# A PSUM pool chosen tile by tile, with a new order of the second part of the program, in a gated linear attention followed by a low-rank mixer

## The chip, the cores and the metric

One core of a Trainium2 chip runs the whole program. The metric is the device time of one execution in microseconds. TensorE (PE in the profile, with its weight loads shown apart as PEld), VectorE (DVE), ScalarE (ACT) and GpSimd (POOL) each take their instructions in program order; SyncE (SP) does nothing but issue transfers, in program order too.

## The reference

Two stages in float32, batch 4, 768 tokens, 8 heads of 48. The first is a gated linear recurrence with a complex gate per channel; the second adds a low-rank mix over the tokens and then a two-layer network with a ReLU.

```python
for t in range(S):                                   # S = 768
    new_re = ar * S_re - ai * S_im                   # ar, ai: normalized gates of token t
    new_im = ar * S_im + ai * S_re
    kv = einsum('bhd,bhe->bhde', k[:, :, t], v[:, :, t])
    S_re, S_im = (new_re + kv, new_im)
    y[:, :, t] = einsum('bhd,bhde->bhe', q[:, :, t], S_re)

x  = y as (B, S, 384)
u  = x + (x^T @ U @ V)^T                             # U 768x32, V 32x768
ch = maximum(u @ w_ch1, 0.0) @ w_ch2                 # 384 -> 1536 -> 384
return u + ch
```

## The kernel before

**Attention.** The tokens are cut into 24 chunks of 128 (6 for each batch), two chunks to a group, and each chunk into two halves of 64 rows (`HC`). What a token gains or loses through the gates is made once for a group: magnitudes and angles on ACT and DVE, sums over tokens as matmuls with constant triangles (`ef ps`, `es ps`, L692; `ph`, L799; `tot`, L744). Then, for each chunk:

- `prep` (L843) weighs q and k, and PE transposes them (`tr`, L866); ACT copies the transposes out of PSUM (L877).
- `chain` (L888) has the scores within blocks of 32 tokens (`inner`, L913 and L916). DVE selects them by masks (L928, into a tile named `DG`), and four transfers that SP issues put the four diagonal blocks into the score matrix `AT` (L964). PE adds the scores across blocks (`corners`, L977), copied by ACT (L982).
- `dk` (L1002) is what the chunk adds to the state `G`; DVE scales and adds it (`onward`, L1008).
- `y` is scores times values (`inside`, L1033, which needs the four transfers) plus queries times state (`before`, L1041).

Four more transfers (L724) lay a group's totals out as `T`; they are issued by SP too.

**Mixer.** Twelve mixers work on two chunks each: `rank` (L1076) and `mixed` (L1095) are the low-rank mix, `uTp` (L1113) the transposes. The first layer is `up` (L1128) in the first three mixers and in the others `few` (L1228), 15 products in place of 18, in groups of 8 matmuls, added together by ACT and DVE (L1236, L1240). The second layer is `down` (L1319 in the first, L1362, seven products in place of eight, in groups of 6, in the others), with the sums by DVE at L1354 and L393. `leave` (L1298) writes the result out.

**How a matmul lies on the array.** Most groups load the whole 128x128 array: `few`, `down`, `up`, `uTp`, `rank`, the sums over tokens. The others load a part: `inside` and `dk` 64x64 pieces, `tr` and `mixed` two halves of 64 rows, `inner`, `corners` and `before` strips of 96 rows by 16, 32 or 64 columns. The argument `way` of a group names this.

**The order.** The body of the program does not issue its operations as it goes. It calls `plan.add` for each (through `PE`, `DVE`, `ACT`, `SP`, `POOL`), and `Plan.order` (L218) sorts all 2770 operations by a table, `ORDER`, that gives each its position. The table has a row for each engine and kind of operation and a list for each chunk, group or mixer, so it sets what stands next to what on every engine, and with that the order of SP's transfers (kinds `load`, `totals` and `place`). Waits between the engines follow from the data and from the buffers.

**PSUM.** There are four pools of two banks: `psT`, `psA`, `psY`, `psM`. Every PSUM tile is taken from one of them, in turn, and the tile that takes a bank waits until the tile two back in the same pool has been read. The pool of a tile is given by its kind: sums over tokens, `rank`, `mixed`, `uTp` and half the transposes in T, `inner`, `corners` and the other half in A, `dk` and most `y` in Y, `up` and `down` in M, and `few` in Y or M for its two long sums and A or T for the rest. The whole program has 479 such tiles.

Of the kernel before, what the change touches and what calls it, by code (L numbers as in the profile page):

```python
# [16 lines left out]
PSUM = bass.MemoryType.PSUM  # L17
# [11 lines left out]

ORDER = {  # L30
# [28 lines left out]
        ('DVE', 'gates'): {0: [5, 8, 13, 18, 19, 54, 49], 1: [30, 21, 40, 43, 44, 51, 50], 2: [111, 143, 156, 185, 169], 4: [277, 322, 323, 372, 356],  # L59
# [10 lines left out]
        ('ACT', 'angles'): {0: [72, 86, 98, 100, 103], 1: [76, 106, 112, 114, 126], 2: [210, 231, 251, 240, 241, 242, 263, 269, 271], 4: [375, 395,  # L70
# [5 lines left out]
        ('DVE', 'angles'): {0: [81, 89], 1: [87, 107], 2: [211, 232, 252], 4: [376, 402, 425], 6: [589, 596, 601, 611, 624, 625, 664], 8: [697, 714,  # L76
# [4 lines left out]
        ('DVE', 'prep'): {0: [85, 104, 110], 1: [121, 128, 145], 2: [226, 250, 265], 3: [203, 304, 309], 4: [373, 424, 427], 5: [443, 470, 472], 6:  # L81
# [6 lines left out]
        ('ACT', 'prep'): {0: [115, 117, 120, 122], 1: [158, 147, 154, 160], 2: [266, 270, 283, 281], 3: [319, 320, 327, 318], 4: [442, 439, 446, 445],  # L88
# [4 lines left out]
        ('DVE', 'rest'): {0: [118, 149, 155, 175, 159, 170, 194], 1: [174, 229, 234, 259, 209, 235, 248, 253], 2: [288, 315, 325, 366, 291, 314, 324,  # L93
# [79 lines left out]
        ('POOL', 'small'): {0: [790, 789], 1: [1213, 993, 1219], 2: [1414, 1280, 1404], 3: [1712, 1508, 1563], 4: [1901, 1754, 1798], 5: [2048, 2010,  # L173
        2037], 6: [2388, 2121, 2330], 7: [2427, 2408, 2409], 8: [2591, 2517, 2557], 9: [2692, 2645, 2657], 10: [2723, 2711, 2745]},
        ('POOL', 'angles'): {6: [614], 8: [706, 731], 10: [875, 913], 12: [1074], 14: [1226, 1309], 16: [1482, 1564], 18: [1745], 20: [1942, 1978],
        22: [2251, 2287]},
        ('DVE', 'mixing'): {3: [868, 1004, 892, 1043, 1073, 822, 1255, 1044, 1266, 1275, 1286, 1298, 1290]},
}
# [1412 lines left out]
```

## Time and profile before

| | |
|---|---|
| time, median of 3 runs | 622.64 us (622.42 to 623.75) |
| the profiled execution | 622.64 us, of which its span 620.9 us |
| granted TensorE clock | 1.00 |
| busy: PE / PEld / DVE / ACT / POOL | 97% / 85% / 86% / 65% / 6% |

The span is what the profile shows, from the first instruction to the last; 1.74 us of the profiled time lie around it. PE is the engine that is busy nearly all the time; DVE is close to that up to about 400 us and has room behind it. PE's first instruction whose place is changed by the table begins at about 170 us.

### The profile page before, as it was taken

To read this page: it belongs to the slowest core of one execution; us is meant where nothing else is said; L and a number is where in the kernel's file an instruction comes from. 1 tells how busy PE (TensorE), PEld (TensorE's weight loads), DVE (VectorE), ACT (ScalarE), POOL (GpSimd) and SP (SyncE) were. 2 spreads that over 40 slices of the span, in tenths; PEclk is the share of its full clock that TensorE was granted. 3 is DMA by queue.
4 is the path that set the end of the run, shared out by engine and by line. 5 is a ranking of instruction groups with operands and counts; after the bars stand their busy time and mean duration, and the time that the engine had idled before them with its cause. 6 is when DMAs were issued, how large, how long until landed. Compare 5 with 4: busy or idle time off the path is not lost.

```text
span 620.9 us, 23949 instructions
## 1 busy us (share of the span) xinstructions
PE 603.4 (97%) x10572; PEld 528.4 (85%) x10572; DVE 531.1 (86%) x967; ACT 403.4 (65%) x789; POOL 36.3 (6%) x76
## 2 busy tenths in 40 slices
PE   6998988999999999999999999999999999999998
PEld 3566767656889889799999999799999998999997
DVE  6999998898999989999999999788789986465553
ACT  6999998889877988596777887566553622202020
POOL 4000000000000010010010100100001000000000
PEclk9999999999999999999999999999999999999999
DMA  9865556645215362530530522421122201000000
GB/s 213 193 146 117 135 117 151 160 100 117 65 20 104 57 120 45 98 76 10 103 79 14 100 64 46 83 60 26 31 57 53 59 5 24 7 21 20 6 20 26
DMA packets 173687, 45.77 MB, mean 74 GB/s; under 512 B 167632, under 2 KB 170384, under 8 KB 173584
## 3 DMA queue, kind: packets, MB, share of 16 engines
q1 hardware_dynamic: 171376, 39.90, 31.4%
q0 software_dynamic: 2208, 4.35, 2.0%
q8 instruction: 83, 1.36, 1.0%
q14 instruction: 20, 0.16, 0.1%
HBM read 33.59 MB, written 4.72 MB: 62 GB/s over the span
## 4 chain that ended last, share of the span: by engine, by line
PE 83%; ACT 10%; DVE 4%; DMA 1%; issue 1%; SPq 1%; ACTq 0%; DVEq 0%
PE down L1362 23%; PE few L1228 20%; PE up L1128 6%; PE tr L866 4%; PE y L1041 3%; PE dk L1002 3%; ACT gate L387 3%; PE inner L916 2%; PE down L1319 2%; PE y L1033 2%; PE inner L913 2%; PE mixed L1095 2%; PE tot L744 2%; ACT QK L877 2%; PE rank L1076 1%
## 5 line engine op out<-in xcount | busy, mean ns | idle before, releaser
L390 DVE TENSOR_TENSOR QK<-QK,T 96x512 f32<-96x512 f32 (+2 forms) x144 | 102.5, 725 | 2.8 <-ACT QK L877 1.1
L1362 PE MATMUL down<-w,h 128*128 128x192 f32 x396 | 73.3, 331 | 0.0
L387 ACT ACTIVATE gate<-gate 128x768 f32<-128x768 f32 (+1 forms) x82 | 64.7, 794 | 5.9 <-DMA gate<-in_a_re_dram 1.8
L1362 PEld LDWEIGHTS down<-w,h 128*128 128x128 f32 x396 | 64.1, 190 | 2.2 <-DVE QK L390 0.6
L1236 ACT COPY h<-few 128x512 f32<-128x512 f32 x54 | 31.5, 585 | 52.4 <-PE few L1228 44.9
L877 ACT COPY QK<-tr 96x512 f32<-96x512 f32 x96 | 51.5, 583 | 12.0 <-PE tr L866 11.6
L393 DVE TENSOR_TENSOR xo<-down,xo 128x192 f32<-128x192 f32 (+1 forms) x79 | 30.1, 385 | 23.8 <-PE down L1362 23.1
L1128 PE MATMUL up<-uT,w 128*128 128x256 f32 x216 | 50.4, 384 | 0.0
L1228 PE MATMUL few<-stage,w 128*128 128x128 f32 x360 | 46.6, 277 | 0.0
L1128 PEld LDWEIGHTS up<-uT,w 128*128 128x128 f32 x216 | 40.0, 190 | 5.5
L1228 PEld LDWEIGHTS few<-stage,w 128*128 128x128 f32 x360 | 43.3, 192 | 0.4
L390 DVE TENSOR_TENSOR QKC<-qk,cs 128x768 f32<-128x768 f32 x44 | 41.6, 951 | 2.0 <-PE dk L1002 1.6
L1240 DVE CUSTOM_DVE_ANT_1 h<-few,h 128x512 f32<-128x512 f32 x54 | 35.7, 685 | 5.9 <-PE few L1228 5.0
L1228 PE MATMUL few<-stage,sums 128*128 128x128 f32 x288 | 38.6, 278 | 0.0
L1362 PE MATMUL down<-stage 128*128 128x192 f32 x198 | 37.4, 330 | 0.0
L1228 PEld LDWEIGHTS few<-stage,sums 128*128 128x128 f32 x288 | 35.0, 192 | 0.7
L781 POOL DMA_DIRECT2D gate<-F x15 | 12.0, 802 | 387.5 <-DVE gate L764 132.2
L982 ACT COPY AT<-corners 32x128 f32<-32x128 f32 x96 | 24.1, 255 | 14.0 <-PE corners L977 12.7
L866 PEld LDWEIGHTS tr<-ident,QKC 64*96 64x96 f32 x768 | 24.7, 123 | 9.8 <-DVE QKC L390 2.3
L1362 PEld LDWEIGHTS down<-stage 128*128 128x128 f32 x198 | 32.1, 190 | 0.7 <-DVE xo L393 0.2
L866 PE MATMUL tr<-ident,QKC 64*96 64x64 f32 x768 | 30.2, 220 | 2.5 <-DVE QKC L390 1.6
L393 DVE TENSOR_TENSOR h<-few,h 128x512 f32<-128x512 f32 x27 | 18.3, 685 | 15.8 <-ACT h L1236 10.4
(195 smaller groups left out, 1353.6 us busy)
## 6 DMA issues: line engine op xcount, KB each, us to landing
stage<-in_moe_w_ch_dram SPq DMA_DIRECT2D x12, 768.0 KB, 5.2
qk<-in_q_dram SPq DMA_DIRECT2D x24, 192.0 KB, 3.7
qk<-in_k_dram SPq DMA_DIRECT2D x24, 192.0 KB, 3.6
VP<-in_v_dram SPq DMA_DIRECT2D x24, 192.0 KB, 4.2
gate<-in_a_re_dram SPq DMA_DIRECT2D x22, 192.0 KB, 3.7
gate<-in_a_im_dram SPq DMA_DIRECT2D x22, 192.0 KB, 4.4
AT<-DG SPq DMA_DIRECT2D x96, 32.0 KB, 2.3
T<-E SPq DMA_DIRECT2D x48, 48.0 KB, 3.0
```

The costliest lines, as they stand in the source:

```text
L387: return nc.scalar.activation(out=o, in_=i, func=f, **kw)
L390: nc.vector.tensor_tensor(out=o, in0=a, in1=b, op=OP.mult)
L393: nc.vector.tensor_tensor(out=o, in0=a, in1=b, op=OP.add)
L866: nc.tensor.transpose(out=get(*ps[r])[0:DQ, h], in_=get(*qkc)[at, h * DQ:(h + 1) * DQ], identity=ident[at, at], tile_position=(r * HC, 0))
L877: nc.scalar.copy(out=to, in_=a)
L982: ACT(0.36, RR, lambda r=r, u=u: nc.scalar.copy(out=get(*ATi).rearrange("p (a u) t -> p a u t", u=2)[r:r + BLK, :, u, BLK:2 * BLK], in_=ge ...
L1002: nc.tensor.matmul(out=get(*dk[r])[x:x + w, h], lhsT=get(*ks)[at, h * DQ + x:h * DQ + x + w], rhs=get(*VPi)[at, h], start=True, stop=True, ...
L1128: nc.tensor.matmul(out=get(*ps)[:, e], lhsT=w1[:, f, (ff + e) * 128:(ff + e + 1) * 128], rhs=get(*uT)[:, f], start=(f == 0), stop=(f == KD ...
L1228: nc.tensor.matmul(out=get(*ps)[:, q], lhsT=w()[:, q * 128:(q + 1) * 128], rhs=v[0](), start=(n == 0 and q == 0), stop=True, skip_group_ch ...
L1236: ACT(c_act(n3 * CH) - 0.045, RU, lambda i=i, k=k: nc.scalar.copy(out=at(i, k), in_=get(*ps)), [ps], [o])
L1240: DVE(c_dve(n3 * CH), RU, lambda i=i, k=k: nc.vector._custom_dve(dve_ops.TENSOR_ADD_SAT, out=at(i, k), in0=get(*ps), in1=at(i, k), s0=math ...
L1362: nc.tensor.matmul(out=get(*to)[:, part], lhsT=x(j), rhs=y[:, j], start=(first and j == 0), stop=(j == KH - 1), skip_group_check=not first)
```

## The change

Two things, which go together.

**The pools.** A string, `BANKS`, names the pool of each PSUM tile by the number at which the program creates it, and `psum` takes that and no longer the kind's pool. The pools themselves stay four of two banks. For the tiles used ahead of the second batch the letter is the one that the kind had; 239 of the 479 tiles get another pool. T has 161 tiles now and had 244, A 117 (109), Y 130 (72), M 71 (54).

**The order.** The positions below 789 of 2770 are as before. Behind them `ORDER` has other numbers for every engine. No operation is added or left out, and each is the same instructions on the same shapes. All later lines of the file are 7 lower down.

```diff
+BANKS = (
+    "TTTTTTTTTTTTTTTTTTAAAAYYYYTTAAAAYYYYTTAAAAYYYYTTAAAAYYYYTTTTTTTTTTAAAAYYYYTTAAAAYYYTTTMMMMMMTTAAYYAATTMMTTTTMMMMMYMMAMAY"
...
 ORDER = {
...
-        21.7: [1789, 1840], 22: [1944], 22.7: [1820, 1797], 23: [1680, 1742, 1780, 1734, 2110], 23.7: [2022, 1970], 24: [2210], 24.7: [1986, 2014],
+        21.7: [1795, 1777], 22: [1850], 22.7: [1798, 1802], 23: [1628, 1660, 1699, 1688, 2041], 23.7: [1945, 2002], 24: [2070], 24.7: [2055, 2046],
...
     def psum(base, tag, shape, padded=None):
-        buffer(base, "ps" + tag, 2, shape, PSUM, padded)
+        buffer(base, "ps" + BANKS[len(wide)], 2, shape, PSUM, padded)
         wide[base] = 0 if padded and len(shape) > 2 else math.prod(shape[1:]) // 128
```

Three places show how the order moves. The first is PE around the last transposes of chunk 18, between `dk` of one chunk and `y` of the next. Before:

```order
L1002 MATMUL dk<-VP_106,QKC_95 48x48
L866 MATMUL tr<-ident,QKC_93 96x64 x16
L1362 MATMUL down<-stage 128x192 x3
L866 MATMUL tr<-ident,QKC_95 96x64 x16
L1033 MATMUL y<-VP_106,AT_111 64x48 x16
L1041 MATMUL y<-GM,QK 64x48 x8
L1041 MATMUL y<-G,QK 64x48 x8
```

And with the change:

```order
L1009 MATMUL dk<-VP_106,QKC_95 48x48
L1369 MATMUL down<-stage,more 128x192 x3
L873 MATMUL tr<-ident,QKC_93 96x64 x16
L873 MATMUL tr<-ident,QKC_95 96x64 x16
L1040 MATMUL y<-VP_106,AT_111 64x48 x16
L1048 MATMUL y<-G,QK 64x48 x8
L1048 MATMUL y<-GM,QK 64x48 x8
```

The two transposes (of q and of k) stand together, and the `down` group that stood between them has moved ahead of both. Over the reordered part of PE's program (534 groups of its 688) the number of neighbours that lie on the array in different ways goes from 172 to 159.

The second is SP where it issues the score blocks of chunks 10 and 11 (`AT_107` and `AT_111`). Before:

```order
L964 DMA AT_107<-DG_108 32x8x32 x4
L543 DMA VP_104<-in_v_dram 128x8x48
L964 DMA AT_111<-DG_112 32x8x32
L724 DMA T_102<-E 48x8x32
L964 DMA AT_111<-DG_112 32x8x32 x3
L534 DMA gate<-in_a_im_dram 128x8x48
```

And with the change:

```order
L971 DMA AT_107<-DG_108 32x8x32 x3
L541 DMA gate<-in_a_im_dram 128x8x48
L971 DMA AT_107<-DG_108 32x8x32
L971 DMA AT_111<-DG_112 32x8x32 x4
L541 DMA gate<-in_a_re_dram 128x8x48
```

A transfer of group 7's totals (`T_102<-E`) stood between the four of chunk 11 and now comes later; the load of a gate has moved in among those of chunk 10.

The third is SP at the score blocks of chunks 16 (`AT_107`) and 17 (`AT_111`). Before:

```order
L964 DMA AT_107<-DG_108 32x8x32 x3
L964 DMA AT_111<-DG_112 32x8x32
L724 DMA T_102<-E 48x8x32
L964 DMA AT_111<-DG_112 32x8x32
L964 DMA AT_107<-DG_108 32x8x32
L724 DMA T_102<-E 48x8x32
```

And with the change:

```order
L971 DMA AT_107<-DG_108 32x8x32 x3
L971 DMA AT_111<-DG_112 32x8x32
L971 DMA AT_107<-DG_108 32x8x32
L971 DMA AT_111<-DG_112 32x8x32 x2
L731 DMA T_102<-E 48x8x32
```

Chunk 16's fourth block no longer stands behind two transfers of totals; chunk 17's next two follow it directly. On DVE the last mask of chunk 16, on which these transfers wait (the row `DG_108` with 8x16), stood here before:

```order
L1240 ISA h<-few,h 128x4x128 x3
L676 TENSOR_TENSOR GS_92<-GL,GS_91 128x768
L928 COPY_PREDICATED DG_108<-mask,inner 128x8x16
L390 TENSOR_TENSOR qk<-qk,es 128x768
L1240 ISA h<-few,h 128x4x128
```

And with the change:

```order
L1247 ISA h<-few,h 128x4x128 x2
L397 TENSOR_TENSOR qk<-qk,es 128x768
L1247 ISA h<-few,h 128x4x128
L935 COPY_PREDICATED DG_112<-mask,inner 128x8x16
L397 TENSOR_TENSOR QK<-QK,T_103 96x16x16
L1361 TENSOR_TENSOR stage<-h 128x384
L935 COPY_PREDICATED DG_108<-mask,inner 128x8x16
```

The second `inner` of chunk 16, which that mask selects from, stands in the table right ahead of the mask before, and between the two instructions of the first row now; so six instructions stand between on DVE.

More of the change, by code (lines that the diff above doesn't have):

```diff
@@ L28 @@
 INV_PI = 0x3EA2F983
+BANKS = (
+    "TTTTTTTTTTTTTTTTTTAAAAYYYYTTAAAAYYYYTTAAAAYYYYTTAAAAYYYYTTTTTTTTTTAAAAYYYYTTAAAAYYYTTTMMMMMMTTAAYYAATTMMTTTTMMMMMYMMAMAY"
+    "YYTTMYMMTTTTTTTTTTTTTTTTTTAAATYYMTTTAAAYTYTAYTMMYAAAATYTTTYAAAATYYTTMMTATYYTYAMTTYYYYMYTYYAAMAYYAATATTTAMMAAYMMAYATTAYYM"
+    "MTMMAYMMTTTMMTTTAAATTATYATTAYATAYMYYATTTYTAYYTTYMATAYMAYAATYTYTMYAATYYMYMMYYYATYATYATAAATTATYAYAYAYTYATYMYATYMYYAYTTTTAA"
+    "TTYMMYYYAAYYTYYYAYYTATYTATATMMAYYATMTAMTMYYYTAYYMMYAYAMYYAMMYTATTTYAYATYTATTTTYATMYMTMTMYYMMTTYATYYMYYTYMATTAAYMAMYYAMA")
 ORDER = {
[1 row of a table removed]
[1 row of a table added]
         97], 2.6: [176], 3: [33, 77, 80, 95], 3.5: [61, 60], 5.1: [124], 5.6: [171], 5.7: [125, 214], 6: [212], 6.1: [267], 6.6: [321], 6.7: [196,
@@ L102 @@
-        ('DVE', 'levels'): {0: [123, 135, 148, 136, 137, 152], 1: [177, 192, 202, 195, 198, 225], 2: [292, 302, 308, 301, 303, 312], 3: [328, 371,
[9 rows of a table removed]
-        ('ACT', 'levels'): {0: [138], 1: [215], 2: [305], 3: [378], 4: [468], 5: [530], 6: [764], 7: [847], 8: [937], 9: [1046], 10: [1177], 11:
[2 rows of a table removed]
[7 rows of a table added]
+        ('DVE', 'levels'): {0: [123, 135, 148, 136, 137, 152], 1: [177, 192, 202, 195, 198, 225], 2: [292, 302, 308, 301, 303, 312], 3: [328, 371,
[9 rows of a table added]
+        ('ACT', 'levels'): {0: [138], 1: [215], 2: [305], 3: [378], 4: [468], 5: [530], 6: [764], 7: [830], 8: [962], 9: [1058], 10: [1175], 11:
[2 rows of a table added]
@@ L115 @@
         ('SP', 'place'): {0: [173, 199, 180, 181], 1: [249, 260, 244, 262], 2: [350, 349, 348, 347], 3: [415, 414, 418, 416], 4: [493, 500, 497, 499],
[4 rows of a table removed]
[4 rows of a table added]
         ('PE', 'rest'): {0: [157, 119, 127, 207, 208], 1: [254, 227, 230, 272, 274, 273], 2: [332, 294, 289, 358, 384, 380], 3: [428, 397, 400, 435,
[6 rows of a table removed]
-        ('ACT', 'rest'): {0: [191, 182, 200, 201, 219, 223, 222], 1: [255, 261, 256, 258, 280, 279, 278], 2: [342, 341, 336, 335, 385, 390, 391], 3:
[10 rows of a table removed]
-        ('ACT', 'small'): {0: [594, 285, 307, 492, 396, 554, 590, 549, 622, 635], 1: [742, 797, 775, 803, 780, 848, 857], 2: [929, 931, 1070, 1069,
[4 rows of a table removed]
@@ L143 @@
-        ('DVE', 'small'): {0: [246, 599, 630, 636, 639, 637, 684, 681, 602, 606, 729, 735], 1: [703, 739, 689, 833, 810, 828, 879, 886, 908, 916, 944,
[29 rows of a table removed]
-        ('POOL', 'small'): {0: [790, 789], 1: [1213, 993, 1219], 2: [1414, 1280, 1404], 3: [1712, 1508, 1563], 4: [1901, 1754, 1798], 5: [2048, 2010,
-        2037], 6: [2388, 2121, 2330], 7: [2427, 2408, 2409], 8: [2591, 2517, 2557], 9: [2692, 2645, 2657], 10: [2723, 2711, 2745]},
-        ('POOL', 'angles'): {6: [614], 8: [706, 731], 10: [875, 913], 12: [1074], 14: [1226, 1309], 16: [1482, 1564], 18: [1745], 20: [1942, 1978],
@@ L176 @@
-        22: [2251, 2287]},
-        ('DVE', 'mixing'): {3: [868, 1004, 892, 1043, 1073, 822, 1255, 1044, 1266, 1275, 1286, 1298, 1290]},
[6 rows of a table added]
+        ('ACT', 'rest'): {0: [191, 182, 200, 201, 219, 223, 222], 1: [255, 261, 256, 258, 280, 279, 278], 2: [342, 341, 336, 335, 385, 390, 391], 3:
[10 rows of a table added]
+        ('ACT', 'small'): {0: [594, 285, 307, 492, 396, 554, 590, 549, 622, 635], 1: [742, 800, 775, 808, 780, 844, 860], 2: [900, 930, 1065, 1076,
[4 rows of a table added]
+        ('DVE', 'small'): {0: [246, 599, 630, 636, 639, 637, 684, 681, 602, 606, 729, 735], 1: [703, 739, 689, 832, 877, 897, 862, 919, 901, 938, 978,
[29 rows of a table added]
@@ new lines @@
+        ('POOL', 'small'): {0: [929, 793], 1: [1101, 1103, 1208], 2: [1514, 1246, 1421], 3: [1726, 1584, 1640], 4: [1867, 1831, 1915], 5: [2198, 1951,
+        2151], 6: [2186, 2266, 2321], 7: [2424, 2353, 2486], 8: [2581, 2503, 2566], 9: [2655, 2617, 2651], 10: [2710, 2678, 2761]},
+        ('POOL', 'angles'): {6: [614], 8: [706, 731], 10: [866, 912], 12: [1057], 14: [1265, 1312], 16: [1448, 1521], 18: [1698], 20: [1950, 2023],
+        22: [2175, 2244]},
+        ('DVE', 'mixing'): {3: [842, 845, 1024, 1078, 1098, 933, 1062, 1026, 1243, 1250, 1268, 1316, 1280]},
```

218 rows, old and new, of the table ORDER are left out of this document.

## The prediction

> **What bounds the kernel now.** I read the page first: busy shares, clock, chain.
>
> ```profile
> span 620.9 us, 23949 instructions
> PE 603.4 (97%) x10572; PEld 528.4 (85%) x10572; DVE 531.1 (86%) x967; ACT 403.4 (65%) x789; POOL 36.3 (6%) x76
> ...
> PEclk9999999999999999999999999999999999999999
> ...
> PE 83%; ACT 10%; DVE 4%; DMA 1%; issue 1%; SPq 1%; ACTq 0%; DVEq 0%
> ```
>
> PE works 97% of the span at the full granted clock, and the chain runs through it for 83%. The change begins on PE at about 170 us, so I asked next for the windows behind that point. The columns are us, then busy time and count of PE, PEld, DVE, ACT and POOL, the clock, the DMA share and GB/s.
>
> ```profile
> 260.00:290.00 30.00, 30.00 (x615) 27.08 (x613) 28.86 (x56) 22.59 (x41) 1.92 (x3) 1.00 0.28 58
> 320.00:350.00 30.00, 30.00 (x517) 29.00 (x515) 29.32 (x58) 22.93 (x44) 0.08 (x1) 1.00 0.22 39
> 530.00:560.00 30.00, 30.00 (x228) 29.49 (x227) 15.77 (x37) 4.85 (x9) 1.62 (x3) 1.00 0.04 14
> 170.00:616.70 446.70, 445.68 (x7865) 417.18 (x7864) 374.64 (x713) 252.20 (x512) 26.20 (x42) 1.00 0.25 49
> ```
>
> In the part that is reordered PE is busy for 445.68 of 446.70 us. All its idle time together is 1.02 us, so the change can't gain more than that by removing waits; it can gain by making PE's own work shorter, or lose by new waits. DVE is nearly as full up to 400 us (29.32 of 30) and half empty behind. The list of waits for the same stretch says what PE, DVE and ACT stood for:
>
> ```profile
> PE y L1033 <- DMA AT<-DG: 0.8, 1, 0.8
> ...
> ACT h L1236 <- PE few L1228: 44.9, 32, 12.1
> ...
> DVE xo L393 <- PE down L1362: 23.1, 19, 3.1
> ```
>
> PE waited once, for a transfer, and never for a bank. The readers of PSUM wait for PE: ACT 32 times for `few`, DVE 19 times for `down`.
>
> **Pools: 0.** A freer choice of banks can only take away waits of PE for the reader of a bank, and there is none. What hides the reuse is that the readers stand ready: ACT has 252.20 us of work in 446.70. If that cover went, PE would wait for one eviction at a time (the page has the copy of `few` at 585 ns). The Trainium skill (Perfetto Trace Analysis, section Matmuls) says that independent groups of matmuls should rotate through different PSUM banks, so that the eviction of one overlaps the matmuls of the next; by it the new pools would pay, but this trace has no such wait left to remove. What the pools do is to permit the other order.
>
> **Neighbours on the array.** The same 534 groups stand in another sequence, and a group takes longer where its neighbour lies on the array in another way. The chain shows `down` and `few` in long rows:
>
> ```profile
> 549.89 11.70 PE down L1362 x72
> 561.59 13.49 PE few L1228 x120
> ```
>
> That is 0.975 us for 6 of `down`. In the timeline of PE I take a group's time from its start to the start of the next:
>
> ```profile
> 305.18 0.71 PE L866 MATMUL tr<-ident,QKC 64*96 64x64 f32 x16
> 305.82 1.24 PE L1362 MATMUL down<-w,stage 128*128 128x192 f32 x6
> 306.90 1.14 PE L1362 MATMUL down<-w,more 128*128 128x192 f32 x6
> 307.96 0.65 PE L866 MATMUL tr<-ident,QKC 64*96 64x64 f32 x16
> 308.55 0.68 PE L1033 MATMUL y<-VP,AT 64*64 64x48 f32 x32
> 309.16 0.67 PE L1041 MATMUL y<-G,QK 96*64 96x48 f32 x16
> 309.66 0.64 PE L1041 MATMUL y<-GM,QK 96*64 96x48 f32 x16
> 310.23 1.14 PE L1002 MATMUL dk<-VP,QKC 64*64 64x48 f32 x64
> ...
> 392.70 1.24 PE L1362 MATMUL down<-stage 128*128 128x192 f32 x6
> 393.88 0.65 PE L866 MATMUL tr<-ident,QKC 64*96 64x64 f32 x16
> ```
>
> A `down` behind a `tr` takes 305.82 to 306.90, 1.08; one with a `tr` on either side takes 392.70 to 393.88, 1.18. So a change between the full array and a part costs about 0.10. One between two kinds of part is cheaper: the second half of `y` takes 0.57 where `dk` follows (309.66 to 310.23) and the first 0.50 where its like follows, 0.07.
>
> The order of the changed kernel says how many of each there are. Fewer: from a full-array group into `dk` or `y` 17 to 10, from `tr` or `mixed` to a full-array group 25 to 14, the other way 22 to 20, from `dk` or `y` into `tr` 5 to 2, and two single ones, 25 in all. More: from `tr` into `dk` or `y` 5 to 9, and eight others among strips and pieces, 12 in all. The `tr` of q and of k, which had a `down` between them, now stand together in several places. So 25 x 0.10 - 12 x 0.07 = 1.7 us less PE work. Bounds: nothing, if a surplus goes with the group and not with its neighbour; at most 13 x 0.20 = 2.6, if the whole surplus of the `down` between two transposes belongs to one change and the rest nets out.
>
> **The one wait.** The timelines of SP and PE around it:
>
> ```profile
> 250.86 0.55 SPq L543 DMA_DIRECT2D VP<-in_v_dram  x1
> 251.50 0.59 SPq L964 DMA_DIRECT2D AT<-DG  x1
> 252.18 1.70 SPq L724 DMA_DIRECT2D T<-E  x1
> 253.93 1.92 SPq L964 DMA_DIRECT2D AT<-DG  x3
> ...
> 259.13 0.92 PE L1033 MATMUL y<-VP,AT 64*64 64x48 f32 x32 [0.82 <-DMA AT<-DG]
> 259.98 0.67 PE L1041 MATMUL y<-G,QK 96*64 96x48 f32 x16
> ```
>
> SP issues chunk 11's first block, then stands 1.70 us at a transfer of totals, then issues the other three; `y` of chunk 11 waits 0.82 for the last, and runs 0.85 where the undisturbed one above takes 0.61. In the new order the four stand in a row, and the transfer of totals behind them. That frees 1.70 and needs 0.82, so the wait goes: 0.82 + 0.24 = 1.06, say 1.0. Late next is the transfer of totals, whose reader is many groups off. Bounds: 1.06, or nothing if a gate load's wait ahead of the four (it has moved in there) holds SP as long.
>
> **New waits.** Chunk 16 is where I find the new order tighter:
>
> ```profile
> 374.23 1.26 PE L913 MATMUL inner<-QK 96*16 96x16 f32 x128
> 375.42 0.86 PE L744 MATMUL tot<-total,GL 128*96 128x32 f32 x8
> ...
> 389.13 0.68 PE L1033 MATMUL y<-VP,AT 64*64 64x48 f32 x32
> ...
> 375.06 0.28 DVE L928 COPY_PREDICATED DG<-mask,inner 128x128 f32<-128x128 int32 x1
> 375.26 0.95 DVE L390 TENSOR_TENSOR qk<-qk,es 128x768 f32<-128x768 f32 x1
> 376.13 0.68 DVE L1240 CUSTOM_DVE_ANT_1 h<-few,h 128x512 f32<-128x512 f32 x1
> ...
> L964 SPq DMA_DIRECT2D AT<-DG x96: 585/608/1945, 36.1 to 516.0; - x96
> ...
> DMA to landing us min/median/max: 1.9/2.3/5.5
> ```
>
> From the end of `inner` to `y` PE had 389.13 - 375.42 = 13.7 us of other work, and has some 8.3 now (seven groups of `down`, one pair of sums, `corners`). Ahead of the mask that `y` needs, DVE now has two of the 0.68, one of the 0.95 and three small ones, some 3.3 us when its ends overlap as above; then the fourth block is the fifth issue, 5 x 0.61, and lands 2.3 later: 3.3 + 3.05 + 2.3 = 8.65, or 0.4 too late. A queue behind that is SP's own: chunk 17's blocks, read some groups later. I add 0.3 for the first 20 us of the new part, where ACT is as closely followed by PE but I find no single row to price. So +0.7, with bounds of 0 and five such waits of 0.8, 4.0.
>
> **Sum.** -1.7 - 1.0 + 0.7 = -2.0 us. The profiled execution took 622.64, its span and 1.74 around it, and that is also the median of the runs; so 622.64 - 2.0 = 620.6 us. The forecast's own range is 619.2 to 622.0.
>
> **Rivals.**
>
> *DVE sets the pace (slower).* In the first two windows above DVE has 0.7 and 1.1 us free in 30, and the new order puts its products with `T` and its masks at other places among the evictions. Place: the `inner` of the 12 chunks 8 to 19, which need QK from DVE's row L390. Price: one operation late, between a mask (0.28) and a product of half size (0.55, as DVE's `stage` takes too), 0.41 in the mean, for each chunk: 4.9 us. With the first two terms, 622.64 - 2.7 + 4.9 = 624.8. It decides once PE waits over 0.22 a chunk. For it: DVE is as full as PE there. Against: before, PE did not wait for DVE once, and what PE takes between a product and its reader is about as long in the new order as in the old. Chance 0.23.
>
> *Nothing comes of it (same).* The surplus goes with the groups, the wait of chunk 11 moves to another chunk (each chunk has four transfers in the same queue), and a small wait is added: 622.3. For it: several of the pairs that go, go because the `down` stands beside another part group now. Chance 0.25.
>
> *A change costs the same drain whatever the two ways are (faster still).* Then each of the 13 that go gives the 0.20 of the bound: -2.6 - 1.0 + 0.7, 619.7. For it: the 1.18. Against: the 0.07 between two parts, and 0.10 for each end of the `down`. Chance 0.18. The Trainium skill (TensorEngine Tiling (Array Packing), section Key Properties) states it as a rule, that changing the tiling mode drains the TensorE; the trace agrees that a change costs, and doesn't show one price for all.
>
> That the change does not do what it says can be left out: both orders hold the same instructions, and the places shown differ.
>
> **How the numbers follow.** Forecast 0.34, DVE 0.23, nothing 0.25, drain 0.18. About 0.2%, 1.25 us, is what a measurement of this kernel can tell from no change. Faster than 621.4: the drain and most of the forecast, 0.50; within: nothing, and the forecast's upper end, 0.26; slower than 623.9: DVE, 0.24 with a little from the bound of 4.0. Range: below, the drain's 619.7 less what the bounds leave under it, 618.3; above, past the DVE rival's 624.8 to 625.6; 1 in 10 lies outside on either side.
>
> **What would show it.** Right: the wait of `y` on `AT<-DG` near 259 us is gone from PE's list; PE's busy time behind 170 us is 1 to 2.5 us less at the same counts; a wait of `y` of chunk 16 under 1 us at most; DVE's list shows no more for PE than before. Wrong: PE's list has waits on QK or on DVE's products between 200 and 400 us (the DVE rival), a wait for a bank (an eviction ahead of a PE group that writes), or the busy time unchanged with only the wait gone (nothing).

## The result and the profile after

| | before | changed |
|---|---|---|
| median, runs side by side | 623.69 us (621.21 to 626.38, 15 runs) | 620.49 us (619.11 to 623.26, 15 runs) |
| ratio | | 0.9947 (95% interval 0.993 to 0.9965) |
| profiled execution | 622.64 us, span 620.9 | 619.11 us, span 616.9 |
| reordered part, from PE's first moved group to its last | 446.5 us | 444.7 us |

The change makes the kernel 3.2 us faster. The page of the changed kernel, lines as shown of before:

```profile
span 616.9 us, 23966 instructions
PE 598.9 (97%) x10572; PEld 526.8 (85%) x10572; DVE 531.5 (86%) x967; ACT 401.8 (65%) x789; POOL 36.3 (6%) x76
...
PEclk8999999999999999999999999999999999999999
...
q8 instruction: 83, 1.36, 1.0%
...
PE 88%; ACT 8%; issue 1%; DVE 1%; DMA 1%; SPq 0%; ACTq 0%
```

PE does the same 10572 instructions in 4.5 us less busy time. The windows from the first moved PE group to the last (us, then busy time and count of PE, PEld, DVE, ACT and POOL) of the changed kernel:

```profile
168.07:612.77 444.70, 442.47 (x7864) 416.19 (x7863) 375.79 (x714) 250.67 (x513) 26.77 (x43) 1.00 0.25 50
```

and PE's list of waits in it:

```profile
PE dk L1009 <- issue: 1.3, 2, 0.8
PE inner L923 <- ACT F L394: 0.4, 1, 0.4
PE tr L873 <- issue: 0.4, 1, 0.4
```

The wait of `y` for the score blocks is gone, and no row names DVE or the reader of the bank that PE takes. The row of `inner` (at 170.25 us) names ACT's `F`, which `inner` does not read and which reads another bank. `F` ended at 170.18 and DVE's product `QK`, which `inner` does read, at 170.11, so that wait may be one for DVE. New are waits put down to "issue", that is, to nothing that the profile shows as a releaser. They stand in the middle of a group. PE's timeline at the longest:

```profile
228.31 0.67 PE L1048 MATMUL y<-GM,QK 96*64 96x48 f32 x16
228.81 0.64 PE L1048 MATMUL y<-G,QK 96*64 96x48 f32 x16
229.37 0.91 PE L1009 MATMUL dk<-VP,QKC 64*64 64x48 f32 x47
231.06 0.45 PE L1009 MATMUL dk<-VP,QKC 64*48 64x48 f32 x17 [0.78 <-issue]
```

47 of the 64 matmuls of `dk` run, then PE stands for 0.78 us, then the other 17. All entries of PE in the trace (weight loads, matmuls, semaphore waits) counted from zero at the program's start, the first entry behind such a gap is number 193 of 256 each time: 7617, 8129 and 13249 are 29, 31 and 51 times 256, plus 193. The page's row `q8 instruction` has 83 packets of 16,384 bytes for the 21,323 entries, one for 256 entries. The last of them ahead of the three gaps began 2.25, 2.63 and 2.39 us before the gap ended. That points to PE standing for its own instructions; the trials with the stream moved, below, bear on it. In the first profile of before no such gap lies in the reordered part.

Taken apart (how, stands ahead of the table below), the part of the two profiles differs by -1.81 us: the wait of `y` -0.96, `inner` waiting for ACT +0.54, the new gaps +2.21, and PE's work -3.60. What of that comes back in other executions, and what each piece of the prediction is worth by itself, was left to trials.

### The profile page after: what moved, and what is told of

Same layout as the page of the kernel before. It is cut to its first block, busy times and chain, and to the rows that moved or that the text cites. A ratio compares the mean times of both kernels' runs of the same rounds, so it can differ in the third digit from the quotient of the medians.

```text
span 616.9 us, 23966 instructions
## 1 busy us (share of the span) xinstructions
PE 598.9 (97%) x10572; PEld 526.8 (85%) x10572; DVE 531.5 (86%) x967; ACT 401.8 (65%) x789; POOL 36.3 (6%) x76
## 4 chain that ended last, share of the span: by engine, by line
PE 88%; ACT 8%; issue 1%; DVE 1%; DMA 1%; SPq 0%; ACTq 0%
PE down L1369 25%; PE few L1235 20%; PE up L1135 7%; PE dk L1009 4%; PE tr L873 4%; PE y L1048 3%; PE inner L923 3%; PE down L1326 2%; PE inner L920 2%; ACT gate L394 2%; PE y L1040 2%; PE tot L751 2%; PE mixed L1102 2%; PE rank L1083 1%; PE es ps L699 1%; PE up L1528 1%
```

## The experiments

For each profile I took the time of each of the 533 PE groups from its start to the start of the next, and off it the tenth percentile of its kind (line and count) in the first profiles of both kernels; that base is 420.80 us for all. What is left is put down to a gap at entry 193, to another wait (over 0.42 us, 0.13 of it left with the neighbour), to a neighbour that lies on the array in another way, or to one that lies alike. Times in us; the ratio is to before, with runs side by side.

| kernel | part | ways differ at | that costs | alike | gaps at 193 | other waits | ratio (95%) |
|---|---|---|---|---|---|---|---|
| before | 446.51 | 172 | 16.95 | 7.80 | 0 | 0.96 | |
| before, again | 448.89 | 172 | 16.95 | 7.79 | 2.32 | 1.03 | 1.0005 (0.9991 to 1.002) |
| chunk 11's transfers | 448.03 | 172 | 17.07 | 7.84 | 2.32 | 0 | 0.9991 (0.997 to 1.0011) |
| old order, new pools | 455.82 | 172 | 18.24 | 8.83 | 2.41 | 5.54 | 1.0107 (1.0087 to 1.0128) |
| the change | 444.70 | 159 | 13.53 | 7.62 | 2.21 | 0.54 | 0.9947 (0.993 to 0.9965) |
| the change, again | 444.78 | 159 | 13.75 | 7.65 | 2.58 | 0 | 0.9941 (0.9924 to 0.9958) |
| new order, old pools | 465.09 | 159 | 15.83 | 11.00 | 0.83 | 16.64 | 1.0282 (1.0262 to 1.0302) |
| 14 groups put apart | 453.84 | 181 | 18.26 | 7.91 | 2.03 | 4.85 | 1.0098 (1.0062 to 1.0134) |
| 8 groups put apart | 448.33 | 172 | 16.60 | 8.20 | 1.84 | 0.90 | 1.002 (0.9997 to 1.0044) |
| stream 52 further | 444.35 | 159 | 13.96 | 7.64 | 1.95 | 0 | 0.9946 (0.9928 to 0.9964) |
| stream 20 further | 444.91 | 159 | 13.68 | 7.36 | 3.07 | 0 | 0.9954 (0.9932 to 0.9976) |
| two groups ahead of dk | 446.43 | 160 | 13.87 | 7.85 | 0.58 | 3.33 | 0.9987 (0.9969 to 1.0004) |

**The two kernels once more.** No edit.

> The changed kernel once more, to see what of its profile comes back. If the gain lies in the reordered part: from PE's first moved group (168.1 us) to its last (612.8 us) it takes 444.7 +- 0.5 us again, against 446.5 in the profile of before. If PE stands for its own instructions there (the three waits put down to 'issue', 0.4, 0.8 and 0.5 us, each at the instruction that is number 193 of a group of 256 in PE's stream), they come back at the same three places. Rival: these waits are chance and come elsewhere. If the 2.1 us by which the unchanged front was shorter are chance, the front is 168 to 170 us; if they belong to the change, 168.1 again.

> Before once more, for its profile. If PE's waits at instruction 193 of 256 belong to the old order too and were missing in its first profile by chance, they stand at the two dk groups where the kernels with the old order had them (357 and 454 us, 0.7 and 1.5 us), and the reordered part takes 447 to 449 us and not 446.5; then the gain of the change in that part is 2.5 to 4 us. Rival: the first profile was typical, no such waits, 446.5. The front 168 to 170 us. Ratio 1.000.

The changed kernel came back to 0.1 us (444.78), with its gaps at the same three entries. Before came out 2.4 us longer than in its first profile, all of it gaps:

```profile
PE dk L1002 <- issue: 1.9, 2, 1.4
PE y L1033 <- DMA AT<-DG: 0.9, 1, 0.9
```

Its timeline has the longer one, in the middle of a `dk` again:

```profile
453.78 0.49 PE L1002 MATMUL dk<-VP,QKC 64*48 64x48 f32 x13
455.68 0.55 PE L1002 MATMUL dk<-VP,QKC 64*48 64x48 f32 x21 [1.40 <-issue]
```

The two other kernels with before's sequence on PE had both gaps too, at the same entries (13249 and 16833). So three of four profiles of that sequence have them and the one that I predicted from did not. Against the second profile the part is 448.9 - 444.75 = 4.1 us shorter, against the first 1.8; the runs say 3.2 (2.2 to 4.4), in between. The gap goes with the start of the last instruction packet ahead of the entry. In the first profile of before the packet ahead of entry 13249 began 0.89 us before PE reached the entry 256 earlier, and the one ahead of 16833 began 1.22 us after; in the three others they began 0.96 to 1.14 and 2.81 to 3.44 us after. Why they start early in one execution and late in another is open. The unchanged front took 170.2 us in the first profile of before and 167.3 to 170.6 in the other eleven; its 2.1 us between the first two profiles were chance.

The windows show the rest of the difference in PE's busy time, 445.86 in the second profile of before:

```profile
168.43:617.31 448.88, 445.86 (x7863) 417.19 (x7862) 374.26 (x712) 252.12 (x512) 26.19 (x42) 1.00 0.24 49
```

That is 3.4 us more than in the changed kernel, for the same instructions.

**Chunk 11's transfers in a row.** Before, with one transfer of totals moved behind them.

```diff
+MOVES = (
+    (1240, 1245),
+)
...
-        for n in sorted(range(len(at)), key=lambda n: at[n]):
+        turn = sorted(range(len(at)), key=lambda n: at[n])
+        for a, b in MOVES:
+            turn.insert(b, turn.pop(a))
+        for n in turn:
```

> Before with one SP operation moved: the transfer of totals that stood between the four score blocks of chunk 11 goes behind them. The prediction's term: y of chunk 11 no longer waits, so 1.0 us less (ratio 0.9984), PE's list without the 0.8. Rival: the wait moves to another y or to the reader of T, ratio 1.000.

SP's timeline has the four together, and `y` starts without a wait:

```profile
250.33 3.28 SPq L972 DMA_DIRECT2D AT<-DG  x4
253.71 0.60 SPq L732 DMA_DIRECT2D T<-E  x1
...
257.34 0.68 PE L1041 MATMUL y<-VP,AT 64*64 64x48 f32 x32
```

The wait did not move elsewhere: 448.03 against 448.89 with the same gaps, 0.9 us. The runs can't tell so little (0.997 to 1.0011); the part of the profile can.

**The pools alone, and the order with the old pools.** The first takes before and gives 197 tiles another pool, the change's wherever the old order permits it: 139 of them get the change's and 58 a third one, which neither kernel gives them; the second takes the change and gives 95 of its 239 tiles the pool of their kind back, as many as the new order permits. The edit is to the letters of `BANKS` alone (before gets the string and the new line in `psum` for it). The last 16 letters of its first line in the change, in the first kernel and in the second:

```diff
-TTTTMMMMMYMMAMAY
+TTTTMMMMMAMMTMAT
```

```diff
-TTTTMMMMMYMMAMAY
+TTTTMMMMMYMMTMTT
```

> The order of before, with another pool for 197 of the 479 PSUM tiles (the pool of the change wherever that order permits it, 353 tiles in all). The prediction's theory, pools alone do nothing: 0 +- 0.5 us, ratio 1.000, no wait for a bank in the list. Rival, the gain comes from the banks being taken more freely: at least half of it, -1.5 us or ratio 0.9975.

> The order of the change, with the pool of the tile's kind given back to 95 of the 239 tiles, as many as the order permits. If the pools do nothing but permit the order: 444.7 +- 1 us in the reordered part. If, as the old order with the new pools shows, a pool that is permitted can still be late, waits for a bank come up on PE's list, 1 to 6 us in all.

Neither came out as nothing. PE's list of the first:

```profile
PE up L1135 <- DVE F L817: 1.5, 1, 1.5
PE inner L923 <- DVE h L1247: 0.7, 1, 0.7
PE dk L1009 <- DVE F L817: 0.7, 1, 0.7
```

`up` has no data from `F`. Its tile got the bank in Y that a sum `ph` had two tiles before, and DVE reads that into `F`. This `ph` is one of the 58: in the change it stands in A, before in T.

```profile
203.26 1.24 PE L1369 MATMUL down<-w,stage 128*128 128x192 f32 x6
206.01 1.35 PE L1135 MATMUL up<-uT,w 128*128 128x256 f32 x5 [1.51 <-DVE F L817]
...
205.41 0.54 DVE L817 SCALAR_TENSOR_TENSOR F<-F,ph 128x384 f32<-128x384 f32 x1
```

The read ends at 205.95 and `up` starts at 206.01. Of the second kernel these are the five longest rows of the list. The `ef ps` of the last row reads nothing of `h`; it got the bank of a `few` sum that DVE reads into `h`.

```profile
PE y L1040 <- ACT QK L884: 1.9, 3, 1.4
PE dk L1009 <- ACT QK L884: 1.8, 2, 1.1
PE tot L751 <- ACT ef L394: 1.2, 2, 1.0
PE tr L873 <- ACT xo L1059: 1.0, 1, 1.0
PE ef ps L699 <- DVE h L1247: 0.9, 1, 0.9
```

An order that permits a pool only says that the reader stands ahead in the program. Whether it has run in time is another matter. With 95 tiles back the new order loses 20.4 us, and with the new pools the old one some 6 us (ratio 1.0107). Neither half brought the gain without the other. No kernel has the old order with the change's pools and nothing else, since that order does not permit them all. So the rival that freer banks alone bring the gain falls for the pools that were tried, and the 6 us are not the price of the change's own pools in the old order.

**Neighbours put apart.** The change with PE groups moved by a few places, so that more of them have a neighbour that lies in another way: 14 groups and 181 such places first, then only the 8 behind which no new wait stood, and 172.

```diff
+MOVES = (
+    (946, 949),
+    (1482, 1487),
+    (2380, 2377),
...
+)
```

> The change with 14 PE groups moved by a few places so that 181 neighbours in the reordered part lie on the array in different ways and not 159, nothing else moved. At the price of the prediction (0.10) it is 22 x 0.10 = 2.2 us slower than the change; at the price that the two profiles give (2.8 us less work for 13 fewer, 0.2 each) 4.4 us. Rival, the surplus goes with the group and not with its neighbour: 0 us. Read from the reordered part: 444.7 us plus that, and the three waits for 'issue' as they are.

> The change with only 8 of the 14 moved groups, those behind which no wait showed: 172 neighbours in different ways, as many as before, instead of 159. At 0.21 each, as the 22 gave, 13 x 0.21 = 2.7 us more PE work; at the prediction's 0.10, 1.3 us; if the neighbours had no price, 0. The reordered part takes 447.4, 446.0 or 444.7 us, plus or minus what the waits for the stream of instructions differ.

With 14 the part grew by 9.1 us, 4.6 of it in what the neighbours cost, (18.26 - 13.64) / 22 = 0.21 for each (13.64 is the mean of the two profiles of the change); most of the rest was waits, for ACT's copy of `corners` above all, so its total proves little. With 8 the count is that of before, and so is nearly the time: the part 448.33 us, PE's busy time 445.84 and the ratio 1.002.

```profile
170.59:618.91 448.32, 445.84 (x7864) 417.12 (x7863) 375.13 (x713) 250.38 (x513) 26.72 (x43) 1.00 0.25 50
```

(16.60 - 13.64) / 13 = 0.23 for each. From before to the change it is (16.95 - 13.64) / 13 = 0.25. Putting 13 neighbours apart takes the gain back: of the 3.6 us by which the part grew, 3.0 lie with them.

**The stream moved.** The idle matmuls of the first 9 us are issued one column block at a time, which adds entries to PE's stream ahead of everything: with 16 blocks in place of 8, 52 more; with the same 8, 20 more.

```diff
-SPARE = {20: 8, 32: 9,
+SPARE = {20: 16, 32: 9,
...
         while run:
-            idle(min(run, AHEAD))
-            run -= min(run, AHEAD)
+            k = min(run, AHEAD if at > 20 else 1)
+            idle(k)
+            run -= k
```

> The change with 13 more idle matmuls in the first 9 us, where PE waits 3.7 us for DVE (16 columns blocks one by one, before it were 8 in three instructions): 52 more entries in PE's stream, so that every later instruction stands 52 further in its group of 256; order, pools and work behind are the same. If PE waits where such a boundary falls into a dense run of small matmuls, the waits move: none at 231 and 359 us, new ones near 219, 242, 305, 317, 363, 456, 487 and 501 us, in all 2 to 8 us in place of 2.2 to 2.6, so the reordered part takes 445 to 450 us; all at entry 193 of 256. Rival: the waits belong to those dk groups (their data, a transfer), and stay where they are, 444.7 us.

> The change with the eight idle column blocks of the first 9 us issued one by one and not in three instructions: the same work, 20 more entries in PE's stream. Waits at entry 193 of 256 move with it: the ones at 231 and 359 us go or shrink, 220 stays, others may come near 243, 305 and 365 us; 1 to 3 us in all, the reordered part 443.5 to 445.5 us. If they were gone altogether: 442.3 us, ratio to before 0.990, the fastest of all. Rival (nothing to do with the stream): 231 and 359 as before.

At 52 the `dk` of chunk 9 runs through:

```profile
227.81 0.64 PE L1048 MATMUL y<-G,QK 96*64 96x48 f32 x16
228.38 1.14 PE L1009 MATMUL dk<-VP,QKC 64*64 64x48 f32 x64
229.45 2.86 PE L1135 MATMUL up<-uT,w 128*128 128x256 f32 x12
```

The gap at 359 us is gone too, the one at 220 stayed within its dense run, and new ones of 0.5 and 0.6 came at 365 and 490, all at entry 193; of the eight places that were expected, 220 among them, three came. At 20 the gap at 359 went, and 248, 311 and 370 came. The one at 231 was expected to go or shrink and did neither (0.91 us idle, 0.78 in the change), but it came ten matmuls earlier in the same `dk`, behind 37 and not 47, which is 20 entries with their weight loads:

```profile
230.23 0.78 PE L1009 MATMUL dk<-VP,QKC 64*64 64x48 f32 x37
231.91 0.57 PE L1009 MATMUL dk<-VP,QKC 64*64 64x48 f32 x27 [0.91 <-issue]
```

So the place is the stream's and not the group's. In both kernels the list puts the gap at 220 down to an ACT instruction, which had ended 0.7 us (at 52) and 0.3 us (at 20) before PE went on. The sizes were 1.95 us at 52, where 2 to 8 was written, and 3.07 at 20, where 1 to 3 was. Neither shift gave a faster kernel.

**A slow group put ahead.** The change with an `up` group ahead of the `dk` of chunk 9 and a `few` group ahead of that of chunk 15, so that PE gets to the entry later.

```diff
+MOVES = (
+    (1136, 1120),
+    (1789, 1787),
+)
```

> The change with two PE groups moved: an up group ahead of the dk of chunk 9 and a few group ahead of the dk of chunk 15, so that the entry 193 of the two dk falls later after the last one. If the waits are for the stream of instructions, the ones at 231 and 359 us go: 1.0 + 0.7 less, 0.2 for neighbours, the part takes 443.2 +- 0.5 us, ratio to before 0.992. Rival: dk's wait is for data, and stays or grows as its readers come 1 to 3 us later: 444.7 or more.

Both gaps went (0.58 us left, at 220), and other waits came in their place, 3.33 us in all:

```profile
PE tr L882 <- DVE QKC L406: 1.6, 1, 1.6
PE few L1244 <- ACT h L1252: 1.1, 1, 1.1
PE inner L932 <- DVE QK L406: 0.4, 1, 0.4
```

`dk` came 2.7 us later, and the next `tr` waited for DVE's `QKC`. That DVE, which reads `dk` and is nearly full there, passed the delay on is the likely reading; no run tests it. That the gaps went fits their cause, and the expected 1.5 us were not to be had this way. No kernel here beats the change.

## Why the prediction was right

**What bounds the kernel.** PE did, and its work could be shortened: of the 4.1 us between the second profiles of both, 3.2 are work (16.95 - 13.75).

**Pools, 0.** Right for the change as made: no wait for a bank ahead of it or behind. The reason given, that the readers stand ready, is too broad: with the same readers, and pools that the order permits but that were not chosen with it, PE waited for banks in both trials. The pools are a condition of the new order, worth up to 20.4 us to it, not a permission that costs nothing.

**Neighbours, -1.7 (0 to -2.6).** The right mechanism and the wrong size: 3.2 to 3.4 us. The step that failed is the price of 0.10. It came from halving the surplus of a `down` between two `tr`, 1.18 - 0.975, and from netting cheap ones against it at 0.07. Where the places were put back, each gave 0.21 and 0.23, near the 0.20 that I had kept for a bound and a rival. One of the signs written down missed for the same reason: PE's busy time behind 170 us fell by some 3 us (3.0 against the first profile of before, 3.4 against the second), where 1 to 2.5 was to show the forecast right.

**The one wait, -1.0.** Right: it is gone in the change, and 0.9 us when only that transfer is moved.

**New waits, +0.7.** `y` of chunk 16 does not wait. DVE ran two of the six instructions ahead of the mask while `inner` still ran, so that the mask ended 1.6 us after `inner` and not 3.3; the fourth block was issued at 381.32 and `y` began at 385.32:

```profile
375.89 1.23 PE L920 MATMUL inner<-QK 96*16 96x16 f32 x128
378.39 0.29 DVE L935 COPY_PREDICATED DG<-mask,inner 128x128 f32<-128x128 int32 x1
378.71 4.53 SPq L971 DMA_DIRECT2D AT<-DG  x7
385.32 0.68 PE L1040 MATMUL y<-VP,AT 64*64 64x48 f32 x32
```

The first 20 us of the part had 0.42 us of wait in one profile and none in the other, about the 0.3. What the step missed are the gaps of the stream, 2.2 to 2.6 us. They did not spoil the sum because before has 2.3 of its own in three of the four profiles of its sequence.

**Sum, -2.0 and 620.6 us.** Measured are -3.2 and 620.49. The time is closer than the difference: before is 623.69 in the longer series and was taken as 622.64. Work that was undersized by 1.6 and gaps that were not thought of stand against each other in the first pair of profiles (-1.8 there). That 620.6 came so near to 620.49 is luck: the difference was 1.2 too small and the time that it was taken from 1.05 too low. What held is the mechanism.

**The rivals.** DVE does not set the pace: no row of PE's list names it, and the one that may hide it is 0.4 us. It is close to doing so, as the wait of `tr` for it with the slow group ahead of `dk` suggests. Nothing comes of it: refuted, the surplus goes with the neighbour. (Its 622.3 does not follow from its own terms either, which take nothing off the 622.64.) The same drain whatever the two ways: its price of 0.20 is what was measured in the mean, but not its form, since in the first profile of before the 18 changes from 64x64 pieces to strips cost 0.04 each and the 12 from pieces to the full array 0.19.

## What to carry to other kernels

Where one engine is full, its order is worth reading as a row of neighbours: the same matmuls took 3.3 us less when 13 fewer of them changed the way they lie on the array. A buffer choice and an order that were made together should be judged together, since one without the other, as far as that could be built, cost 6 to 20 us here. And before a sum is made against one profile, take a second: gaps that stand in three profiles of four were absent in the one used.

## What the runs showed of the hardware

PE can run out of its own instructions, as the gaps that moved with the stream show. They come in packets of 16,384 bytes, one for 256 entries of the trace, and in eleven of the twelve profiles PE stood in the reordered part at the entry that begins such a block, 26 times for over 0.4 us, where some 60 blocks begin in each. Every one of the 26 gaps ended 2.2 to 2.8 us after the last packet's start, and they came in runs of small matmuls or right behind one (64 in 1.07 us is 128 entries). The Trainium skill (Runtime: NRT & Kernel Launch, section Instruction fetch mechanics) has the blocks of 16 KiB and 256 instructions, with which this agrees, and says that crossing one is mostly hidden; here up to 5 of some 60 were not, at 0.3 to 1.6 us each.
